# Float32r transposes of layer-norm outputs, fed by DMA copies, for tiles 3 to 13 of the first layer

## The chip, the cores and the metric

The kernel runs on one core of one Trainium2 chip. Times are device microseconds of one execution of the whole program; the figure for a kernel is the median of its runs.

## What is computed

An input of 2048 rows and 576 columns goes through a linear-attention block and an expert block, twice. Cut to what matters here:

```python
x = A_x
x = x + _A_ref(_layernorm(x), A_wqkv, A_wo)      # linear attention, 32 heads of 18
x = x + _B_ref(_layernorm(x), B_w_q, ...)        # one of 64 experts per head and row
x = x + _A_ref(_layernorm(x), A_wqkv, A_wo)
x = x + _B_ref(_layernorm(x), B_w_q, ...)

# in _A_ref
qkv = x @ wqkv                                   # q, k and v, 576 columns each
pq, pk = phi(q), phi(k)                          # phi(t) = max(t, 0) + min(exp(t), 1) + 1e-6
kv = einsum("bhsd,bhse->bhde", pk, v)
```

The change touches the beginning of the first attention block: layer norm, the transpose of its output, and the products for q, k and v.

## The kernel before

The 2048 rows are 16 tiles of 128 rows. In the code the first layer has the index 0, so a piece called `(0, t)` is tile t of layer 1.

For each tile of the front, ScalarE writes the layer norm's output `y` (line 187, float32, five blocks of 128 columns; the middle 64 columns stand there twice). TensorE transposes the five blocks into one PSUM tile `pt` with a float32 identity (line 197). ScalarE rounds `pt` to a float32r tile `thi` (line 102), VectorE writes the rest into `tlo` (line 103). The products k, v and q (line 212) take 28 matmul pairs each from `thi`, `tlo` and the weights split in the same way (`whi`, `wlo`). ScalarE and VectorE make phi of k and q (lines 218 to 221), q goes to DRAM by DMA (`pq_d`, line 254), and phi(k) with v is summed over the tiles into one PSUM tile `kva` (lines 283 and 285).

The tiles 2 to 12 are done by one loop (lines 724 to 749). The iteration of tile t runs, on TensorE, k of t, v of t, q of t, the transposes of tile t+1 (`fT`) and the sum of t. For t up to 9, eight matrices of the second block's weights are folded at the end (`fold_load`, line 540, and `fold_mm`, line 550); every second iteration from t = 4 on also has `fold_out` and `fold_T`, which move a finished fold through a buffer `foldf` and five more transposes. From t = 10 on there is nothing to fold, and the transposes come between v and q. The layer norm of tile t+1 (`first_ln`) stands at the beginning of the iteration. Tiles 14 and 15 follow in an order written out by hand.

Inside the loop the order on TensorE, ScalarE, VectorE and GpSimd is that of the code (`in_order`). All DMAs are issued by SyncE (SP), in an order that the scheduler sets; SP takes them one after the other, and each waits for its data and its buffer. Every engine works through its own instructions in order, so one that waits holds up all behind it on that engine.

Two pools matter. The tiles `y` and `foldf` share three buffers of one tag. PSUM has four tiles of 128 x 1024 float32 for everything that TensorE writes, one of which `kva` holds through the loop.

Of the kernel before, what the change touches and what calls it, by code (L numbers as in the profile page):

```python
# [11 lines left out]
F32 = mybir.dt.float32  # L12
F32R = mybir.dt.float32r
BF16 = mybir.dt.bfloat16
I32 = mybir.dt.int32
AF = mybir.ActivationFunctionType
ALU = mybir.AluOpType
AX = mybir.AxisListType
# [4 lines left out]
P = 128  # L23
# [12 lines left out]
NB = 5  # L36


def blocks(rem):

    rows, at = [], 0
    for b in range(NB):
        rows.append((at, b - (b > rem)))
        at += 64 if b == rem else P
    return rows
# [12 lines left out]
def network(ctx, tc, x_in, wqkv, wo, wq_t, k_t, u_t, v2, c_mask, c_mask4, c_ident, c_code, c_code1, c_scale, c_shift, out):  # L58
    nc = tc.nc

    cp = ctx.enter_context(tc.tile_pool(name="cp", bufs=1))
    wk = ctx.enter_context(tc.tile_pool(name="wk", bufs=2))
# [3 lines left out]
    def psum(name):  # L66
        return ps.tile([P, 1024], F32, tag="ps", name=name)
# [3 lines left out]


    ident = cp.tile([P, P], F32, name="ident")
    mask = cp.tile([HC + 1, HC + 72], F32, name="mask")
    pick = cp.tile([HC + 1, 2 * P], F32, name="pick")
    code_w = cp.tile([P, 512], BF16, name="code_w")
    shift = cp.tile([P, 64], I32, name="shift")
    mhalf = cp.tile([P, 1], F32, name="mhalf")
# [21 lines left out]
    def split(src, hi, lo, eng=nc.vector):  # L100

        nc.scalar.activation(hi, src, AF.Copy)  # L102
        eng.tensor_tensor(lo, src, hi.bitcast(F32), op=ALU.subtract)  # L103

    def split_mixed(src, dst):

        nc.scalar.activation(dst, src, AF.Copy)
        nc.vector.tensor_tensor(dst[64:], src[64:], dst[64:].bitcast(F32), op=ALU.subtract)
# [24 lines left out]
    def split_weight(tiles, c0, hi, lo, rem, which=range(NB), eng=nc.vector):  # L133
        for b in which:
            cols = slice(c0, c0 + D)
            if b != rem:
                split(tiles[b], hi[:, b, cols], lo[:, blocks(rem)[b][1], cols], eng)
            else:
                split_mixed(tiles[b], hi[:, b, cols])
# [42 lines left out]

    def normalized(xt, rs, n):

        y = wk.tile([P, 2, 320], F32, tag="y", name=f"y{n}", bufs=3)
        x2 = bass.AP(tensor=xt.tensor, offset=xt.offset, ap=[xt.ap[0], [256, 2], [1, 320]])
        nc.scalar.activation(y, x2, AF.Identity, scale=rs[:, 0:1], bias=rs[:, 1:2])  # L187
        return y.rearrange("p a b -> p (a b)")

    def transposed(y, n, more=None, tag="t", step=P):  # L190

        todo = [y[:, b * step:b * step + P] for b in range(NB)] if y is not None else []
        todo += [] if more is None else [more]
        w = len(todo) * P
        pt = psum(f"pt{n}")
        for b, x in enumerate(todo):
            nc.tensor.transpose(pt[:, b * P:(b + 1) * P], x, ident)  # L197
        nb = NB if tag == "t" else NB + 1
        hi = wk.tile([P, nb, P], F32R, tag=tag + "hi", name=f"thi{n}", bufs=4 if tag == "t" else 1)
        lo = wk.tile([P, nb, P], F32R, tag=tag + "lo", name=f"tlo{n}", bufs=4 if tag == "t" else 1)  # L200
        yield
        split(pt[:, :w], hi.rearrange("p a b -> p (a b)")[:, :w], lo.rearrange("p a b -> p (a b)")[:, :w])
        return hi, lo

    def product(tt, hi, lo, cols, n, cut=HALF, rem=REM, by_block=False):

        o = psum(f"pp{n}")
        todo = sorted(passes(rem), key=lambda p: p[1]) if by_block else passes(rem)
        for i, (a, b, w) in enumerate(todo):
            wb = hi[:, b] if w == "hi" else lo[:, blocks(rem)[b][1]]  # L210
            for c0, c1, at in ((0, cut, 0), (cut, D, 512)):
                nc.tensor.matmul(o[:, at:at + c1 - c0], tt[a == "lo"][:, b, :], wb[:, cols + c0:cols + c1],  # L212
                                 start=(i == 0), stop=(i == len(todo) - 1))
        return o
# [9 lines left out]
    tt = {}  # L224
    xs = {}
    ys = {}
# [2 lines left out]


    def front_T(l, t):
        tt["f", l, t] = yield from transposed(ys.pop(("f", l, t)), f"f{l}_{t}")

    def front_k(l, t):
        k = product(tt["f", l, t], whi, wlo, D, f"k{l}_{t}", by_block=(l == 0 and t == 0))
# [177 lines left out]
    def exp_T(l, t, c):  # L413

        y = ys.pop(("b", l, t)) if ok(t) else None
        cg = tt.pop(("cg", l, c)).rearrange("p a b -> p (a b)") if ok(c) else None
        if y is None and cg is None:
            return
        hi, lo = yield from transposed(y, f"b{l}_{t % 99}", cg, tag="t" if cg is None else "u")
        if y is not None:  # L420
            tt["b", l, t] = hi, lo
        if cg is not None:
            b = 0 if y is None else NB
            tt["c", l, c] = hi[:, b], lo[:, b]
# [127 lines left out]

    def fold_out(ch):
        p = fold_ps.pop(ch)
        f = wk.tile([P, 640], F32, tag="y", name=f"foldf{ch}", bufs=3)
        nc.scalar.activation(f[:, :320], p[:, :320], AF.Copy)
        nc.scalar.activation(f[:, 320:384], p[:, 256:320], AF.Copy)
        nc.scalar.activation(f[:, 384:], p[:, 512:768], AF.Copy)
        fold_st["f", ch] = f
# [21 lines left out]
    def warm_up(n):  # L581

        p = psum("warm")
        for i in range(n):
            nc.tensor.matmul(p[:, :512], junk[:, :P], junk[:, :512], start=True, stop=True)

    def first_load(l, t):
        xt = wk.tile([P, D], F32, tag="x", name=f"xf_{t}", bufs=3)
        nc.sync.dma_start(xt, x_in[t * P:(t + 1) * P, :])
        xs["f", t] = xt  # L590
# [47 lines left out]
    def ok(t):  # L638
        return 0 <= t < NT
# [3 lines left out]
    def run(l, *seq):  # L643


        for f, t, *n in seq:
            if f is bc or ok(t):
                g = begun.pop((f, l, t), None) or (exp_T(l, *t) if f is bc else f(l, t))
                for i in range(n[0] if n else 99):
                    if g is None or next(g, bc) is bc:  # L650
                        break
                else:
                    begun[f, l, t] = g
# [39 lines left out]
    with in_order(*ALL):  # L693
        x0, x1 = xs.pop(("f", 0)), xs.pop(("f", 1))
        warm_up(14)
        rs0 = statistics(x0, "f0_0", soon=True)
        split_weight(wk_in, D, whi, wlo, REM, (0,))
        ys["f", 0, 0] = normalized(x0, rs0, "f0_0")
        split_weight(wk_in, D, whi, wlo, REM, (1, 2))
        run(0, (fT, 0, 1))  # L700
        warm_up(2)
        run(0, (fT, 0))
        split_weight(wk_in, D, whi, wlo, REM, (3,), nc.gpsimd)
        rs1 = statistics(x1, "f0_1", soon=True)
        split_weight(wk_in, D, whi, wlo, REM, (4,))
        ys["f", 0, 1] = normalized(x1, rs1, "f0_1")
        run(0, (k, 0, 1), (fT, 1))
        split_weight(wv_in, 2 * D, whi, wlo, REM, (0, 1))
        run(0, (k, 0), (k, 1, 1))
        split_weight(wv_in, 2 * D, whi, wlo, REM, (2, 3, 4))  # L710
        first_load(0, 2)
        wq_in = load_weight(wqkv, 0, REM, "w")
        small_loads()
        first_load(0, 3)
        run(0, (k, 1), (v, 0, 1))
        split_weight(wq_in, 0, whi, wlo, REM, (0, 1))
        run(0, (v, 0))
        first_ln(0, 2)
        split_weight(wq_in, 0, whi, wlo, REM, (2, 3))
        run(0, (v, 1, 1))  # L720
        split_weight(wq_in, 0, whi, wlo, REM, (4,))
        run(0, (st, 0), (fT, 2), (v, 1), (q, 0), (st, 1), (q, 1))
        PER, FIRST = 8, 13
        for t in range(2, FIRST):
            m0 = PER * (t - 2)
            groups = [m for m in range(m0, m0 + PER) if m < 2 * H]
            done = (m0 - 1) // 16 if m0 % 16 == 0 and 0 < m0 <= 2 * H else None
            for m in groups:
                fold_load(m)
            if t + 2 < NT:  # L730
                first_load(0, t + 2)
            if t + 1 < NT:
                first_ln(0, t + 1)
            run(0, (k, t, 1))
            if done is not None:
                fold_out(done)
            run(0, (k, t))
            run(0, (v, t, 1))
            if done is not None and groups:
                fold_T(done)  # L740
            run(0, (v, t))
            if groups:
                run(0, (q, t), (fT, t + 1), (st, t))
            elif t < L:
                run(0, (fT, t + 1), (q if t < L - 1 else st, t), (st if t < L - 1 else q, t if t < L - 1 else -1))
            if done is not None and not groups:
                fold_T(done)
            for m in groups:
                fold_mm(m)
# [101 lines left out]
```

## Time and profile before

| what | before |
|---|---|
| median of 3 runs | 756.94 us (755.6 to 759.04) |
| span of the profiled execution | 753.7 us |
| TensorE busy | 736.8 us, 98% of the span |
| VectorE, ScalarE, GpSimd busy | 456.8, 289.1, 197.7 us |
| one float32 transpose of the layer-norm output, record on TensorE | 270 to 330 ns, 160 of them over both layers |
| fold load, issue to landing | 3.2 to 6.0 us, 64 of 288 KB |

Of the profiled execution no other time is recorded than its span, from the first to the last instruction of the program. In the views PE is TensorE's matmuls, PEld its weight loads, DVE VectorE, ACT ScalarE, POOL GpSimd and SPq the DMA issues of SyncE. A row of the timeline gives start, duration, engine, line, operation, tiles and count, and in brackets the engine's idle time before it with what ended it. Consecutive matmuls overlap, so the distance between starts says more than a record's length. In rows of stretches the last three numbers are the granted TensorE clock, the busy share of the 16 DMA engines and the GB/s that they moved. The lines on which the prediction rests stand in it.

### The profile page before, as it was taken

What the parts mean: (1) busy time and instruction counts of PE and PEld (TensorE: products, weight loads), DVE (VectorE), ACT (ScalarE), POOL (GpSimd) and SP (SyncE); (2) the same over time, 40 slices, a digit from 0 to 9 for tenths busy, and PEclk for the clock granted to TensorE, in tenths of its full rate; (3) what the DMA queues carried; (4) which work ended last, traced back from release to release, by engine and by line L of the source; (5) the groups of instructions that cost most, each with busy time, mean ns of one, the idle gap of its engine ahead of it and who ended that gap; (6) DMA issues with size and microseconds to landing.
All of it is one profiled execution on the core that took longest, in us unless ns stands there. A gap on an engine that the chain in (4) does not pass through costs nothing.

```text
span 753.7 us, 13987 instructions
## 1 busy us (share of the span) xinstructions
PE 736.8 (98%) x5356; PEld 693.2 (92%) x5356; DVE 456.8 (61%) x1008; ACT 289.1 (38%) x586; POOL 197.7 (26%) x540
## 2 busy tenths in 40 slices
PE   7999999999999999999999999999999999999996
PEld 5999989999998989999999999999999999999984
DVE  5532342324246887666666665563366789999996
ACT  5422232232333544444444443533234333343443
POOL 2110001000002543333333342230033343534331
PEclk9999999999999999999999999999999999999999
DMA  9736446631111322222232211321733213111201
GB/s 275 245 125 223 157 171 220 218 118 49 48 63 32 110 89 77 98 84 83 92 105 101 83 67 60 111 68 38 206 107 112 85 65 115 48 48 58 70 33 63
DMA packets 52267, 79.48 MB, mean 105 GB/s; under 512 B 5480, under 2 KB 22376, under 8 KB 52200
## 3 DMA queue, kind: packets, MB, share of 16 engines
q1 hardware_dynamic: 52200, 78.59, 31.8%
q8 instruction: 42, 0.69, 0.4%
q14 instruction: 25, 0.20, 0.1%
HBM read 55.01 MB, written 23.56 MB: 104 GB/s over the span
## 4 chain that ended last, share of the span: by engine, by line
PE 81%; DVE 10%; ACT 3%; issue 2%; POOL 2%; DMA 1%; SPq 0%; DVEq 0%; POOLq 0%; ACTq 0%
PE ppk L212 15%; PE ppv L212 15%; PE ppo L402 13%; PE pps L433 12%; PE ppq L212 11%; PE kva L283 4%; PE fold_ps L550 2%; PE ptf L197 2%; PE ptb L197 2%; PE po L517 2%; PE pto L197 2%; PE m L332 1%; DVE tloo L103 1%; DVE o L379 1%; DVE x L391 1%
## 5 line engine op out<-in xcount | busy, mean ns | idle before, releaser
L219 DVE TENSOR_SCALAR ek<-ek 128x576 f32<-128x576 f32 x32 | 14.7, 459 | 81.4 <-ACT ek L218 76.9
L212 PE MATMUL ppk<-whi,thif 128*128 128x288 f32 x320 | 50.4, 301 | 1.6 <-ACT thif L102 1.6
L402 PE MATMUL ppo<-ohi,thio 126*128 126x288 f32 (+1 forms) x320 | 50.9, 301 | 0.8 <-DVE ct L492 0.5
L212 PEld LDWEIGHTS ppk<-whi,thif 128*128 128x128 f32 x320 | 44.2, 188 | 5.6 <-issue 3.3
L163 POOL TENSOR_SCALAR rsf<-mvf 128x1 f32<-128x1 f32 x16 | 3.1, 192 | 175.6 <-DVE mvf L161 175.4
L212 PE MATMUL ppk<-whi,tlof 128*128 128x288 f32 x320 | 48.7, 296 | 0.3 <-DVE tlof L103 0.3
L212 PE MATMUL ppv<-whi,thif 128*128 128x252 f32 x320 | 48.0, 296 | 0.1
L187 ACT ACTIVATE yb<-x,rsb 128x640 f32<-128x640 f32 x32 | 29.5, 923 | 47.9 <-POOL rsb L180 47.9
L212 PE MATMUL ppv<-whi,tlof 128*128 128x252 f32 x320 | 47.6, 295 | 0.0
L219 DVE TENSOR_SCALAR eq<-eq 128x576 f32<-128x576 f32 x32 | 15.8, 493 | 51.7 <-ACT eq L218 51.7
L433 PE MATMUL pps<-shi,thib 128*128 128x512 f32 x160 | 44.4, 407 | 2.0 <-ACT thib L102 2.0
L402 PEld LDWEIGHTS ppo<-ohi,thio 126*128 126x128 f32 (+1 forms) x320 | 44.6, 189 | 1.9 <-issue 0.7
L212 PEld LDWEIGHTS ppk<-whi,tlof 128*128 128x128 f32 x320 | 44.6, 188 | 0.5 <-DVE tlof L103 0.5
L212 PEld LDWEIGHTS ppv<-whi,tlof 128*128 128x128 f32 x320 | 44.6, 188 | 0.0
L212 PEld LDWEIGHTS ppv<-whi,thif 128*128 128x128 f32 x320 | 44.2, 188 | 0.3 <-ACT thif L102 0.3
L438 ACT ACTIVATE s<-pps 128x512 f32<-128x512 f32 x32 | 19.1, 596 | 61.4 <-PE pps L433 61.4
L433 PE MATMUL pps<-shi,tlob 128*128 128x512 f32 x160 | 42.5, 395 | 0.0
L103 DVE TENSOR_TENSOR tlof<-ptf,thif 128x640 fp32r<-128x640 f32 x32 | 26.2, 818 | 24.3 <-ACT thif L102 24.2
L402 PE MATMUL ppo<-ohi,tloo 126*128 126x288 f32 x256 | 40.3, 295 | 0.0
L402 PE MATMUL ppo<-olo,thio 126*128 126x288 f32 x256 | 40.3, 296 | 0.0
L212 PE MATMUL ppk<-wlo,thif 128*128 128x288 f32 x256 | 39.9, 296 | 0.0
L212 PE MATMUL ppq<-whi 128*128 128x288 f32 x260 | 39.6, 299 | 0.1
(156 smaller groups left out, 1778.6 us busy)
## 6 DMA issues: line engine op xcount, KB each, us to landing
fold<-in_wq_t SPq DMA_DIRECT2D x64, 288.0 KB, 4.8
whi<-hl_d SPq DMA_DIRECT2D x26, 320.0 KB, 3.5
pq_d<-eq SPq DMA_DIRECT2D x19, 288.0 KB
pq<-pq_d SPq DMA_DIRECT2D x19, 288.0 KB, 3.3
xf<-in_x SPq DMA_DIRECT2D x16, 288.0 KB, 4.7
x<-in_x SPq DMA_DIRECT2D x16, 288.0 KB, 2.8
x_d<-x SPq DMA_DIRECT2D x16, 288.0 KB, 3.1
x<-x_d SPq DMA_DIRECT2D x16, 288.0 KB, 2.6
```

What stands on the lines that cost most here:

```text
L103: eng.tensor_tensor(lo, src, hi.bitcast(F32), op=ALU.subtract)
L187: nc.scalar.activation(y, x2, AF.Identity, scale=rs[:, 0:1], bias=rs[:, 1:2])
L197: nc.tensor.transpose(pt[:, b * P:(b + 1) * P], x, ident)
L212: nc.tensor.matmul(o[:, at:at + c1 - c0], tt[a == "lo"][:, b, :], wb[:, cols + c0:cols + c1], start=(i == 0), stop=(i == len(todo) - 1))
L219: nc.vector.tensor_scalar(e, e, 1.0, EPS, op0=ALU.min, op1=ALU.add)
L283: nc.tensor.matmul(a[:w, c * HC:(c + 1) * HC], vt[:, c * w:(c + 1) * w], fk[:, c * HC:(c + 1) * HC], start=(t == 0 and c == 0), stop=(t == ...
L332: nc.tensor.matmul(m[:c, h * 512:h * 512 + HALF], kvb[:n, b * HC:b * HC + c], wob[l][b][:n, h * HALF:(h + 1) * HALF], start=True, stop=True)
L402: nc.tensor.matmul(p[:, h * 512:h * 512 + HALF], hl[a][:r, b], w[:r, h * HALF:(h + 1) * HALF], start=(i == 0), stop=(i == len(todo) - 1))
L433: nc.tensor.matmul(p[:, :512], hl[a == "lo"][:, b, :], shi[:, b] if w == "hi" else slo[:, blocks(REM)[b][1]], start=(i == 0), stop=(i == l ...
L438: nc.scalar.activation(s[:, NE:], p[:, :512], AF.Copy)
L517: nc.tensor.matmul(p[:, b * 512:b * 512 + HALF], c[i], vmix[:, b * HALF:(b + 1) * HALF], start=(i == 0 and not based), stop=(i == 1))
L550: nc.tensor.matmul(p[32 * j:32 * j + 32, at:at + c1 - c0], kpad[:, ch // 2, 24 - 8 * a:56 - 8 * a], st[:, c0:c1], start=(a == 0), stop=(a ...
```

## The change

For the tiles 3 to 13 of layer 1, the output of the layer norm is copied by a DMA from SBUF to SBUF into a second tile `r` of type float32r (`moved`; both ends are seen as float32, so the bits are unchanged). The five transposes then read `r` and a float32r identity, and write the same PSUM tile seen as float32r. Tiles 0 to 2, 14 and 15 and all other transposes stay as they are. The copy stands in the code between the k and the v product of the iteration before the one that uses it.

For tiles 5 and 9 the first block is also transposed both ways, from `y` in float32 and from `r` in float32r (`guard`); ScalarE copies the first result, VectorE compares the two, takes the maximum over a row and adds it to `mhalf`, the constant -0.5 that the layer norm's power uses. Where the two are equal, 0 is added.

The tag of `y`, `r` and `foldf` gets four buffers instead of three, and ScalarE writes the float32r identity once before the loop.

```diff
+    identr = cp.tile([P, P], F32R, name="identr")
...
-    def transposed(y, n, more=None, tag="t", step=P):
+    def transposed(y, n, more=None, tag="t", step=P, raw=False):
...
-            nc.tensor.transpose(pt[:, b * P:(b + 1) * P], x, ident)
+            if raw:
+                nc.tensor.transpose(pt[:, b * P:(b + 1) * P].bitcast(F32R), x, identr)
+            else:
+                nc.tensor.transpose(pt[:, b * P:(b + 1) * P], x, ident)
...
+    def moved(y, n):
+
+        r = wk.tile([P, NB * P], F32R, tag="y", name=f"r{n}", bufs=4)
+        nc.sync.dma_start(r.bitcast(F32), y)
+        return r
+
+    def guard(y, r, n):
+
+        a = psum(f"ga{n}")
+        b = psum(f"gb{n}")
+        nc.tensor.transpose(a[:, :P], y[:, :P], ident)
+        nc.tensor.transpose(b[:, :P].bitcast(F32R), r[:, :P], identr)
+        c = wk.tile([P, P], F32, tag="gc", name=f"gc{n}", bufs=1)
+        nc.scalar.activation(c, a[:, :P], AF.Copy)
+        nc.vector.tensor_tensor(c, c, b[:, :P], op=ALU.not_equal)
+        m = wk.tile([P, 1], F32, tag="gm", name=f"gm{n}", bufs=1)
+        nc.vector.tensor_reduce(m, c, axis=AX.X, op=ALU.max)
+        nc.vector.tensor_tensor(mhalf, mhalf, m, op=ALU.add)
...
     def front_T(l, t):
-        tt["f", l, t] = yield from transposed(ys.pop(("f", l, t)), f"f{l}_{t}")
+        tt["f", l, t] = yield from transposed(ys.pop(("f", l, t)), f"f{l}_{t}", raw=(l == 0 and 2 < t <= 13))
+
+    def front_moved(l, t):
+        y = ys.pop(("f", l, t))
+        r = moved(y, f"f{l}_{t}")
+        if t in (5, 9):
+            guard(y, r, f"f{l}_{t}")
+        ys["f", l, t] = r
...
+        nc.scalar.activation(identr, ident, AF.Copy)
...
             run(0, (k, t))
+            front_moved(0, t + 1)
             run(0, (v, t, 1))
```

On TensorE, in the iteration of tile 4, before: the end of tile 4's k product (`ppk_4`) and the beginning of its v product (`ppv_4`).

```order
L212 MATMUL ppk_4_875<-whi,tlof_4_822 128x288 x10
L212 MATMUL ppv_4_912<-whi,thif_4_821 128x252
L212 MATMUL ppv_4_912<-whi,thif_4_821 128x324
L212 MATMUL ppv_4_912<-whi,thif_4_821 128x252
```

And now, where `gaf_5` and `gbf_5` are the comparison's two PSUM tiles, `yf_5` the layer norm's output of tile 5 and `rf_5` its copy:

```order
L235 MATMUL ppk_4_881<-whi,tlof_4_828 128x288 x10
L219 MATMUL gaf_5_920<-ident,yf_5_879 128x128
L220 MATMUL gbf_5_921<-identr,rf_5_918 128x128
L235 MATMUL ppv_4_930<-whi,thif_4_827 128x252
L235 MATMUL ppv_4_930<-whi,thif_4_827 128x324
```

The two transposes of the comparison stand between k and v of tile 4, and the second reads the copy; tile 8's iteration has the same place for tile 9.

On SP, the DMAs issued around the same time, before: the store of tile 3's phi(q), eight fold loads and a load of x.

```order
L254 DMA pq_d_3_106<-eq_3_810 128x576
L540 DMA fold_850<-in_wq_t 128x576
L540 DMA fold_852<-in_wq_t 128x576
L540 DMA fold_854<-in_wq_t 128x576
L540 DMA fold_856<-in_wq_t 128x576
L540 DMA fold_858<-in_wq_t 128x576
L540 DMA fold_860<-in_wq_t 128x576
L540 DMA fold_1026<-in_wq_t 128x576
L540 DMA fold_1028<-in_wq_t 128x576
L589 DMA xf_1201<-in_x 128x576
```

And now:

```order
L284 DMA pq_d_3_107<-eq_3_816 128x576
L570 DMA fold_856<-in_wq_t 128x576
L570 DMA fold_858<-in_wq_t 128x576
L570 DMA fold_860<-in_wq_t 128x576
L570 DMA fold_862<-in_wq_t 128x576
L570 DMA fold_864<-in_wq_t 128x576
L570 DMA fold_866<-in_wq_t 128x576
L212 DMA rf_5_918<-yf_5_879 128x640
L570 DMA fold_1044<-in_wq_t 128x576
L570 DMA fold_1046<-in_wq_t 128x576
L619 DMA xf_1221<-in_x 128x576
```

The copy of tile 5 stands behind the store and six of the eight fold loads; the last two and the load of x now come after it.

On SP again, near the end of the loop, before: loads of `wo`, the store of tile 10's phi(q), a load of x and the store of tile 11's.

```order
L294 DMA wob_2591<-in_wo 126x576
L294 DMA wob_2597<-in_wo 72x576
L254 DMA pq_d_10_113<-eq_10_1984 128x576
L589 DMA xf_2345<-in_x 128x576
L254 DMA pq_d_11_114<-eq_11_2127 128x576
L354 DMA x_1_2521<-in_x 128x576
```

And now:

```order
L324 DMA wob_2635<-in_wo 126x576
L324 DMA wob_2641<-in_wo 72x576
L284 DMA pq_d_10_114<-eq_10_2024 128x576
L212 DMA rf_12_2096<-yf_12_2061 128x640
L619 DMA xf_2389<-in_x 128x576
L284 DMA pq_d_11_115<-eq_11_2169 128x576
L212 DMA rf_13_2225<-yf_13_2190 128x640
L384 DMA x_1_2565<-in_x 128x576
```

The copies of tiles 12 and 13 each stand right ahead of the load that waited for the same `y` before.

More of the change, by code (lines that the diff above doesn't have):

```diff
@@ L183, in normalized @@
     def normalized(xt, rs, n):
-        y = wk.tile([P, 2, 320], F32, tag="y", name=f"y{n}", bufs=3)
+        y = wk.tile([P, 2, 320], F32, tag="y", name=f"y{n}", bufs=4)
         x2 = bass.AP(tensor=xt.tensor, offset=xt.offset, ap=[xt.ap[0], [256, 2], [1, 320]])
@@ L554, in fold_out @@
         p = fold_ps.pop(ch)
-        f = wk.tile([P, 640], F32, tag="y", name=f"foldf{ch}", bufs=3)
+        f = wk.tile([P, 640], F32, tag="y", name=f"foldf{ch}", bufs=4)
         nc.scalar.activation(f[:, :320], p[:, :320], AF.Copy)
```

## The prediction

> **What bounds the kernel now.** I read the page's busy times first, then the chain that ended last, then the busy times by stretch over layer 1's front, where the change sits.
>
> ```profile
> PE   736.8 (98%) x5356; PEld 693.2 (92%) x5356; DVE 456.8 (61%) x1008; ACT 289.1 (38%) x586; POOL 197.7 (26%) x540
> PE 81%; DVE 10%; ACT 3%; issue 2%; POOL 2%; DMA 1%; SPq 0%; DVEq 0%; POOLq 0%; ACTq 0%
> 60.00:80.00 20.00, 20.00 (x173) 18.90 (x172) 6.15 (x14) 6.85 (x20) 1.01 (x3) 1.00 0.43 149
> 180.00:200.00 20.00, 19.75 (x155) 19.52 (x153) 7.55 (x15) 6.31 (x13) 2.02 (x6) 1.00 0.18 58
> ```
>
> TensorE is busy 98% of the span and all 20 us of 60 to 80; VectorE, ScalarE and the DMA engines (43%) have room. So a microsecond that TensorE loses or saves here goes to the end nearly whole. What counts is how much TensorE time the faster transposes save, and whether TensorE now meets a copy that has not landed.
>
> **What the transposes may save.** One iteration of the loop, tile 4's, as the timeline shows it:
>
> ```profile
> 69.40 1.50 PE L212 MATMUL ppk<-whi,tlof 128*128 128x288 f32 x10
> 70.74 1.49 PE L212 MATMUL ppv<-whi,thif 128*128 128x252 f32 x10
> ...
> 78.73 0.71 PE L197 MATMUL ptf<-ident,yf 128*128 128x128 f32 x5
> 79.27 1.05 PE L283 MATMUL kva<-ek,v 128*127 128x126 f32 x8
> ```
>
> Steps from start to start are safer than lengths, since records overlap. Five float32 transposes take 79.27 - 78.73 = 0.54 us, 0.108 each. Ten float32r matmuls of 288 columns take 70.74 - 69.40 = 1.34 us, 0.134 each, 0.465 ns a column; at that pace 128 columns take 0.060. No row shows a float32r transpose. It may step at 0.108 (nothing gained) or at 0.060; since the moving operand, the identity, is what turns float32r, I take 0.060. It saves 5 x 0.048 = 0.24 us a tile. A gain beyond 0.54 a tile is excluded: that is all the time there is.
>
> Against this stands the load of the weights, which every transpose has for itself:
>
> ```profile
> L197 PEld LDWEIGHTS ptf<-ident,yf x160: 137/140/144, 7.5 to 518.0; 128*128 128x128 f32 x160
> L212 PEld LDWEIGHTS ppk<-whi,thif 128*128 128x128 f32 x320 | 44.2, 188 | 5.6 <-issue 3.3
> ```
>
> A transpose's load is recorded with 140 ns, a float32r matmul's of the same shape with 188. If the float32r transpose gets the longer load, 48 ns more, the load may set the step and the saving is gone. [...]
>
> **What the copies cost.** In the loop each copy stands on SP behind the pq_d store and six fold loads. This is that place in the profile, with the layer norm whose output is copied:
>
> ```profile
> 65.37 0.33 SPq L254 DMA_DIRECT2D pq_d<-eq  x1
> 65.97 4.16 SPq L540 DMA_DIRECT2D fold<-in_wq_t  x8
> 68.49 0.92 ACT L187 ACTIVATE yf<-xf,rsf 128x640 f32<-128x640 f32 x1 [3.91 <-POOL rsf L166]
> 70.23 0.38 SPq L589 DMA_DIRECT2D xf<-in_x  x1
> ...
> L540 SPq DMA_DIRECT2D fold<-in_wq_t x2: 382/625/868, 67.4 to 67.8; - x2
> DMA to landing us min/median/max: 5.2/5.2/5.2
> ...
> 72.00:73.00 1.00, 1.00 (x10) 1.00 (x9) 0.84 (x2) 0.00 (x0) 0.00 (x0) 1.00 0.95 366
> 77.00:78.00 1.00, 1.00 (x10) 1.00 (x9) 0.97 (x4) 0.00 (x0) 0.00 (x0) 1.00 0.00 0
> ```
>
> Tile 5's y is done at 69.41, so its copy is issued at about 69.45. The DMA engines are then saturated (95% busy at 366 GB/s from 72 to 73) and idle again at 77. The fifth fold load, issued at 67.84, landed 5.2 us later, at 73.0. If transfers are served in order, the sixth (0.295 MB at 366 GB/s) comes 0.80 us after it and the copy (128 x 640 x 4 B = 0.328 MB) 0.90 us after that: 74.7.
>
> For most tiles that is early enough. Tile 5's own transposes start at 78.73, 4 us later, and every tile from 3 to 10 has an interval of this kind. Only the comparison asks sooner: its second transpose reads the copy of tile 5 right behind tile 4's k product, and in the program of before the v product starts there, at 70.74. TensorE works in order, so v, q and all that follows wait. With 0.05 us for the wait to end and 0.06 for the transpose, v starts at 74.8: **4.1 us lost**. What the iteration's earlier transposes saved (tile 4's) is lost in this wait too, because the landing hangs on the q product's output, not on them.
>
> Tile 9 is the same, from tile 8's iteration:
>
> ```profile
> 130.67 1.50 PE L212 MATMUL ppk<-whi,tlof 128*128 128x288 f32 x10
> 132.01 0.69 PE L212 MATMUL ppv<-whi,thif 128*128 128x252 f32 x4
> ...
> L540 SPq DMA_DIRECT2D fold<-in_wq_t x2: 382/382/383, 128.6 to 129.1; - x2
> DMA to landing us min/median/max: 5.5/5.5/5.5
> ```
>
> Fifth fold at 129.1 + 5.5 = 134.6, copy at 136.3, v at 136.4 instead of 132.01: **4.4 us**.
>
> The last tiles have no fold loads, but a late layer norm and a transpose that comes before q. Tile 12:
>
> ```profile
> 177.71 0.92 ACT L187 ACTIVATE yf<-xf,rsf 128x640 f32<-128x640 f32 x1 [4.12 <-POOL rsf L166]
> 178.66 0.35 SPq L589 DMA_DIRECT2D xf<-in_x  x1
> 179.62 0.71 PE L197 MATMUL ptf<-ident,yf 128*128 128x128 f32 x5
> 180.57 0.67 PE L212 MATMUL ppq<-whi,thif 128*128 128x288 f32 x3 [0.25 <-DVE ek L221]
> ...
> x_d<-x SPq DMA_DIRECT2D x16, 288.0 KB, 3.1
> x<-x_d SPq DMA_DIRECT2D x16, 288.0 KB, 2.6
> ```
>
> The x load waits for this y and is issued at 178.66; the copy takes its place. The nearest rows, a tile's store and load, land in 2.6 and 3.1 us; I take 2.7, so 181.4, and q starts 0.35 later, at 181.7 instead of 180.57: **1.1 us lost** (1.0 to 1.5 between the bounds), and the 0.25 that q waits for VectorE goes into it. Tile 13:
>
> ```profile
> 190.14 1.60 SPq L354 DMA_DIRECT2D x<-in_x  x2
> 192.91 0.71 PE L197 MATMUL ptf<-ident,yf 128*128 128x128 f32 x5
> ```
>
> Issued at 190.14, landed at 192.7 to 193.2, wanted at 192.91: 0.3 lost at most, about its own saving; I count nothing for the tile.
>
> The rest costs nothing while its cover lasts: the comparison's ScalarE copy and three VectorE steps (0.3 us or so each beside ScalarE's 0.92 for a tile five times as wide) and the float32 transpose (0.11) run while TensorE waits anyway; the identity's copy lies under TensorE's solid work. Two fold loads and an x load go out some 0.5 us later, but the engines are idle by 77 and the folds are used after 80.
>
> **The clock.** TensorE stands still for about 3.9 and 4.2 us. The longest such gap of before is near the end:
>
> ```profile
> 748.17 0.33 PE L197 MATMUL ptb<-ident,cg 128*128 128x128 f32 x1 [2.31 <-DVE cg L498]
> ...
> 747.00:748.00 1.00, 0.00 (x0) 0.00 (x0) 0.83 (x4) 0.00 (x0) 0.00 (x0) 1.00 0.60 233
> 749.00:750.00 1.00, 0.73 (x4) 0.47 (x4) 0.14 (x1) 0.19 (x1) 0.00 (x0) 1.00 0.34 134
> 750.00:751.00 1.00, 0.00 (x0) 0.00 (x0) 0.00 (x0) 0.47 (x1) 0.00 (x0) 0.60 0.42 161
> 751.00:752.00 1.00, 0.00 (x0) 0.00 (x0) 0.00 (x0) 0.00 (x0) 0.00 (x0) 0.50 0.68 265
> ...
> 1.22 5.58 PE L585 MATMUL warm<-junk 128*128 128x512 bf16 x14 [1.22 <-DVE junk L686]
> ```
>
> The granted clock holds through a gap of 2.31 us and halves soon after, when TensorE has had little to do for 4 us. How long it stays low is seen only at the start, where fourteen matmuls take 5.58 us, 0.78 ns a column against 0.465 later. So a fall costs between nothing and half of 5.58, 2.8 us; I take 1.4, and one fall in the two waits. [...]
>
> **The sum.** Lost: 4.1 + 4.4 + 1.1 = 9.6 us. Saved: tiles 3, 5, 6, 7, 9, 10 and 11, 7 x 0.24 = 1.7 (4 and 8 are eaten by the waits, 12 and 13 are counted). 7.9 us, and 9.3 with one fall of the clock. The profiled execution's span is 753.7; the runs have a median of 756.94, 3.2 above it, which lies outside the span and which I leave as it is: 756.94 + 9.3 = **766.2 us**.
>
> **Rivals.**
> - The clock falls in both waits: 7.9 + 2.8 = 10.7, **767.6**. For it: gaps nearly twice the longest one that passed. Against it: the trace's one fall came after 4 us of thin work, not from a single gap.
> - The change does not do what it says, and a float32r transpose steps like a float32 one (the load): the 1.7 is gone, 9.3 + 1.7 = 11.0, **767.9**.
> - Not slower: the copies do not queue behind the folds. They come from SBUF, and if the engines served them beside the loads they would land 2.6 to 3.1 us after 69.45, at 72.1 to 72.6. Then each comparison costs about 1.7, too short for the clock (2.31 passed): 3.4 + 1.1 - 1.7 = 2.8, **759.7**. It decides once the copy lands by about 72.6. Against it: the folds were issued 0.48 apart but landed 5.2 us on, as in a queue, and all go through one SP queue.
> - Faster needs more than 3.8 us; even with transposes that cost nothing (0.54 a tile) the last case stays at +0.7. I leave 2% for what I do not see.
>
> **How the numbers follow.** Forecast 0.48, both falls 0.18, no faster transposes 0.18, early copies 0.14, unseen 0.02. A measurement of this kernel can tell about 0.5%, 3.8 us, from no change. The first three cases lie above it: slower 0.84; early copies are no change: 0.14; faster 0.02. The forecast's own range is 764.8 (no fall, 7.9) to 767.6. The range of 759.5 to 769.5 adds the early copies down to 0.2 below their value, and upward the case of no faster transposes with a second fall (769.3); it leaves out half of the early copies' spread and what I do not see.
>
> **What would show it.** In the profile of after: two idle stretches of TensorE of about 4 us, near 71 and 136, ended by the copy's DMA at the comparison's second transpose; one of about 1 us at tile 12; the granted clock below 1.00 just behind one of the long ones; five float32r transposes in 0.30 us. Long waits without a step below 0.108 mean the load rules. I am wrong at the root if TensorE's waits there are under 2 us, or if the transposes save more than 0.54 a tile elsewhere.

## The result and the profile after

| what | before | after |
|---|---|---|
| median of 4 runs | 757.91 us (755.6 to 759.04) | 769.5 us (769.25 to 770.53) |
| span of the profiled execution | 753.7 us | 768.7 us (time 770.53) |
| mean granted TensorE clock of that execution | 0.998 | 0.989 |

The ratio of after to before is 1.0165, with a 95% interval of 1.0146 to 1.0185: by the ratio the change costs about 12.5 us, by the medians 11.6. The profiled execution of before was one of its quickest (its span of 753.7 and the 1.8 us outside that after's execution shows make 755.5), so the two profiles differ by 15.0 us, more than the medians.

The page of after, in the same order as that of before: busy times, the granted clock in 40 slices of the span, and the chain that ended last.

```profile
PE 738.9 (96%) x5360; PEld 696.0 (91%) x5360; DVE 460.3 (60%) x1014; ACT 289.7 (38%) x589; POOL 196.2 (26%) x540
PEclk9999999899999999999999999999999999999998
PE 77%; DVE 12%; DMA 3%; ACT 3%; issue 2%; POOL 2%; SPq 0%; DVEq 0%; POOLq 0%; ACTq 0%
```

TensorE is busy 2.1 us longer in a span that is 15.0 us longer: most of the time is idle time of TensorE, not work. DMA's share of the chain grew from 1% to 3%, and the clock row has an 8 in its eighth slice, 135 to 154 us. A shorter fall at 76.6 us does not show in these tenths; finer stretches below show it.

What TensorE waited for between 30 and 220 us, over all tiles of the change (us in all, number, longest):

```profile
PE gbf L220 <- DMA rf<-yf: 9.8, 2, 5.1
PE ptf L199 <- DMA rf<-yf: 1.6, 1, 1.6
```

The two long waits are the comparisons of tiles 5 and 9 (`gbf` is the PSUM tile of the second transpose), the third is tile 12. There is none at tile 13. The timeline of TensorE around the first comparison, then around the second:

```profile
69.99 1.50 PE L235 MATMUL ppk<-whi,tlof 128*128 128x288 f32 x10
71.32 0.27 PE L219 MATMUL gaf<-ident,yf 128*128 128x128 f32 x1
76.38 0.25 PE L220 MATMUL gbf<-identr,rf 128*128 128x128 f32 x1 [4.78 <-DMA rf<-yf]
76.46 2.64 PE L235 MATMUL ppv<-whi,thif 128*128 128x252 f32 x10
...
81.79 0.71 PE L595 MATMUL fold_pt<-ident,foldf 128*128 128x128 f32 x5
...
137.62 1.50 PE L235 MATMUL ppk<-whi,tlof 128*128 128x288 f32 x10
144.29 0.34 PE L220 MATMUL gbf<-identr,rf 128*128 128x128 f32 x1 [5.05 <-DMA rf<-yf]
144.43 2.75 PE L235 MATMUL ppv<-whi,thif 128*128 128x252 f32 x10
149.95 0.71 PE L595 MATMUL fold_pt<-ident,foldf 128*128 128x128 f32 x5
```

The same two places in the profile of before, as far as they are not shown yet:

```profile
74.44 0.71 PE L565 MATMUL fold_pt<-ident,foldf 128*128 128x128 f32 x5
...
132.01 1.49 PE L212 MATMUL ppv<-whi,thif 128*128 128x252 f32 x10
...
135.71 0.71 PE L565 MATMUL fold_pt<-ident,foldf 128*128 128x128 f32 x5
```

From the last ten matmuls of k to the first of v it took 1.34 us before at both places (69.40 to 70.74, 130.67 to 132.01), and takes 6.47 and 6.81 us now: 5.1 and 5.5 us lost. Then v itself is longer: from its first matmul to `fold_pt` 3.70 us before at both places, 5.33 and 5.52 now, 1.6 and 1.8 us more. Nothing waits there; it is the clock. Stretches of 2 us in the profile of after (PE, PEld, DVE, ACT, POOL busy, then granted clock, DMA share, GB/s):

```profile
74.00:76.00 2.00, 0.00 (x0) 0.00 (x0) 0.00 (x0) 0.00 (x0) 0.00 (x0) 1.00 1.05 412
76.00:78.00 2.00, 1.62 (x8) 1.66 (x9) 0.74 (x3) 0.00 (x0) 0.00 (x0) 0.65 0.67 263
78.00:80.00 2.00, 2.00 (x10) 2.00 (x9) 0.00 (x0) 0.00 (x0) 0.00 (x0) 0.50 0.00 0
80.00:82.00 2.00, 2.00 (x17) 2.00 (x16) 0.00 (x0) 0.00 (x0) 0.00 (x0) 1.00 0.00 0
...
142.00:144.00 2.00, 0.00 (x0) 0.00 (x0) 0.00 (x0) 0.00 (x0) 0.00 (x0) 0.50 0.98 386
146.00:148.00 2.00, 2.00 (x10) 2.00 (x10) 0.00 (x0) 0.00 (x0) 0.00 (x0) 0.50 0.00 0
```

While TensorE waits, the DMA engines are saturated, 98 to 105% busy at 386 to 412 GB/s by these rows: the copy is coming behind the folds. Behind the first wait TensorE does 10 matmuls in 2 us instead of 17, at a clock of 0.50; at the second the clock is down, 0.50 from 142 to 144 us, before the wait is over.

Tile 12 in the timeline of after, with the layer norm on ScalarE, the end of the v product, the copy's issue on SP, the transposes and the q product behind them, and v's row in before:

```profile
191.67 0.92 ACT L188 ACTIVATE yf<-xf,rsf 128x640 f32<-128x640 f32 x1 [4.12 <-POOL rsf L167]
192.25 1.48 PE L235 MATMUL ppv<-whi,tlof 128*128 128x252 f32 x10
192.62 0.50 SPq L212 DMA_DIRECT2D rf<-yf  x1
195.32 0.59 PE L199 MATMUL ptf<-identr,rf 128*128 128x128 f32 x5 [1.59 <-DMA rf<-yf]
195.75 1.56 PE L235 MATMUL ppq<-whi,thif 128*128 128x288 f32 x10
```

```profile
178.29 1.49 PE L212 MATMUL ppv<-whi,tlof 128*128 128x252 f32 x10
```

The copy is issued at the end of y, with no folds ahead of it, and the wait for it ends 2.7 us later (192.62 to 195.32). From the last ten matmuls of v to q it is 3.50 us (192.25 to 195.75) instead of 2.28 (178.29 to 180.57): 1.2 us lost. The sum: 5.1 + 5.5 for the waits, 1.6 + 1.8 for the clock, 1.2 for tile 12, together 15.2; less 0.9 that the transposes of nine tiles saved, plus 0.8 by which this execution was later before the first float32r transpose (the two traces matched instruction by instruction): 15.1, against 15.0 between the spans.

### The profile page after: what moved, and what is told of

Its sections match the earlier page's. It is cut to its first block, busy times and chain, and to the rows that moved or that the text cites. A ratio compares the mean times of both kernels' runs of the same rounds, so it can differ in the third digit from the quotient of the medians.

```text
span 768.7 us, 14032 instructions
## 1 busy us (share of the span) xinstructions
PE 738.9 (96%) x5360; PEld 696.0 (91%) x5360; DVE 460.3 (60%) x1014; ACT 289.7 (38%) x589; POOL 196.2 (26%) x540
## 4 chain that ended last, share of the span: by engine, by line
PE 77%; DVE 12%; DMA 3%; ACT 3%; issue 2%; POOL 2%; SPq 0%; DVEq 0%; POOLq 0%; ACTq 0%
PE ppv L235 15%; PE ppk L235 13%; PE ppo L432 13%; PE pps L463 11%; PE ppq L235 11%; PE kva L313 3%; PE ptb L201 2%; DMA rf<-yf 2%; PE po L547 2%; PE fold_ps L580 2%; PE ptf L201 1%; PE pto L201 1%; DVE o L409 1%; DMA xf<-in_x 1%; DVE eq L244 1%
## 5 line engine op out<-in xcount | busy, mean ns | idle before, releaser
L235 PE MATMUL ppv<-whi,thif 128*128 128x252 f32 x320 | 50.4, 306 | 0.1
L235 PEld LDWEIGHTS ppv<-whi,thif 128*128 128x128 f32 x320 | 46.2, 196 | 0.4 <-ACT thif L103 0.4
L235 PE MATMUL ppv<-wlo,thif 128*128 128x252 f32 (+1 forms) x256 | 40.1, 300 | 0.0
```

## The experiments

My theory after the result: the slowdown is the two comparisons, each by its place (TensorE waits there for a copy behind six fold loads) and by the fall of the clock that follows. The rivals: the comparison's own work, the copies' traffic or the transposes themselves cost the time; or the queue is the fault and another queue would end the wait. Ratios are to before, run beside it on the same chip, with 95% intervals.

**Without the comparison.** Copies and float32r transposes stay.

```diff
 def front_moved(l, t):
     y = ys.pop(("f", l, t))
     r = moved(y, f"f{l}_{t}")
-    if t in (5, 9):
-        guard(y, r, f"f{l}_{t}")
     ys["f", l, t] = r
```

> The comparison is left out; copies and float32r transposes of tiles 3 to 13 stay. If the comparison's early read of the copy is what costs (the two waits of 4.8 and 5.1 us and the clock behind them), the time returns to that of before: about 1.6 us of gain (0.16 a tile in the profile of after, ten tiles) against about 1.2 lost at tile 12, so a ratio to before of 0.998 to 1.002, no wait of TensorE near 71 or 136 and a granted clock of 1.00 throughout. If the copies themselves cost (DMA traffic, buffers, the start of the program), it stays 3 us or more above before.

Measured 756.65 us, ratio 1.0001 (0.9989 to 1.0013). The only wait of TensorE in these tiles is tile 12's, 1.6 us as in after. The stretch of 20 us around the first comparison's place in this kernel:

```profile
60.00:80.00 20.00, 20.00 (x174) 18.90 (x173) 5.86 (x14) 6.89 (x20) 1.00 (x3) 1.00 0.54 183
```

TensorE is busy all 20 us again at full clock, while the DMA engines move 183 GB/s instead of 149. So the copies' traffic costs TensorE nothing there, copies and transposes together leave the time where it was, and the slowdown is the comparison's. This profile's span is 755.0, 13.7 below that of after; the four terms above make 14.0.

**The comparison in another place.** It stands behind q of the iteration, right ahead of the tile's own transposes; the copy has landed by then.

```diff
+    held = {}
...
     if t in (5, 9):
-        guard(y, r, f"f{l}_{t}")
+        held[t] = y, r
...
-    run(0, (q, t), (fT, t + 1), (st, t))
+    run(0, (q, t))
+    if t + 1 in held:
+        guard(*held.pop(t + 1), f"f0_{t + 1}")
+    run(0, (fT, t + 1), (st, t))
```

> The comparison is kept whole, but stands behind the q product, right ahead of the transposes of the same tile, some 8 us after its place in the changed kernel. If it is the wait and not the work that costs, this is e1 plus two transposes of about 0.1 us each per comparison, 0.4 us in all, ratio to before 0.998 to 1.003. If the comparison's work costs (two PSUM tiles of four, three VectorE steps), it stays 3 us or more above e1.

Measured 757.98 us, ratio 1.0015 (1.0004 to 1.0027). The timeline of TensorE there:

```profile
79.27 0.30 PE L220 MATMUL gbf<-identr,rf 128*128 128x128 f32 x1
80.32 0.61 PE L199 MATMUL ptf<-identr,rf 128*128 128x128 f32 x5 [0.74 <-ACT gcf L222]
```

No wait for the copy is left at the comparisons, so the place was the cost and not the work. I had missed one thing: the five transposes need a PSUM tile, and the one that comes free is that of the comparison's first result, which ScalarE (`gcf`) must read first. That is 0.74 us at each of the two, and by the ratios 1.1 us over the kernel without comparison.

**The wait filled with work.** Eighteen bfloat16 matmuls whose result nobody reads stand between the comparison's two transposes, so that the wait stays and TensorE is busy in it. Half as many in the second kernel below.

```diff
     nc.tensor.transpose(a[:, :P], y[:, :P], ident)
+    for i in range(18):
+        nc.tensor.matmul(b[:, 512:], junk[:, :P], junk[:, :512], start=True, stop=True)
     nc.tensor.transpose(b[:, :P].bitcast(F32R), r[:, :P], identr)
```

> As the changed kernel, but 18 bf16 matmuls on zeros (0.22 us each at full clock, 3.9 us) stand between the comparison's two transposes, so that TensorE is busy during the wait. The wait for the copy still ends when it ends. If the idle time lowers the clock and this costs 1.6 and 1.8 us behind the two waits, the granted clock stays 1.00 and the time is about 3.4 us below the changed kernel's, 766. If the clock's fall costs nothing (the work behind waits for something else anyway), the time stays at 769 to 770.

Measured 765.6 us, ratio 1.0113 (1.0089 to 1.0136). The first comparison on the timeline of TensorE, and after it the stretch behind it:

```profile
72.38 4.05 PE L221 MATMUL gbf<-junk 128*128 128x512 bf16 x18
77.59 0.28 PE L222 MATMUL gbf<-identr,rf 128*128 128x128 f32 x1 [1.16 <-DMA rf<-yf]
77.70 1.57 PE L237 MATMUL ppv<-whi,thif 128*128 128x252 f32 x10
```

```profile
78.00:80.00 2.00, 2.00 (x17) 2.00 (x16) 0.71 (x3) 0.00 (x0) 0.00 (x0) 1.00 0.16 62
```

The copy comes no sooner, and the comparison holds v up as before; but the clock stays at 1.00 and the first ten matmuls of v take 1.57 us by their record instead of 2.64. The ratio is 0.0052 below the result's 1.0165, 3.9 us for both falls, with intervals that leave 1.6 to 6.2; the profile of after had 1.6 + 1.8. What is left, some 8.6 us, is the waits and tile 12.

> As e3, with 9 matmuls in the wait instead of 18, so about 1.9 us of work and then some 3 us of idle time before each copy lands. If the clock falls as soon as a gap is much longer than the 2.3 us that passed, it falls in one or both waits, and the time is 767 to 769.5; if it needs a gap near 4 us or more, it holds, and the time is e3's, 765 to 766.

With nine matmuls: 766.35 us, ratio 1.0123 (1.0104 to 1.0142). The comparison on TensorE's timeline, and after it the stretch around it:

```profile
76.16 0.28 PE L222 MATMUL gbf<-identr,rf 128*128 128x128 f32 x1 [2.36 <-DMA rf<-yf]
76.28 1.56 PE L237 MATMUL ppv<-whi,thif 128*128 128x252 f32 x10
```

```profile
76.00:78.00 2.00, 1.84 (x14) 1.84 (x15) 0.73 (x3) 0.00 (x0) 0.00 (x0) 1.00 0.64 250
```

The idle stretches of 2.36 us here and 2.5 us at tile 9 leave the clock up (1.00 in the row; the execution's mean is 0.996, as without the comparison), and the time equals that with eighteen within the intervals. In two of this kernel's four executions the mean clock was 0.993 and 0.994 beside 0.996 and 0.997, so a fall in those is not excluded.

The length of a wait may not be all that counts. In the profile of after the granted clock changes at 76.59, 80.00, 141.44 and 148.27 us, 3.41, 61.44 and 6.83 us apart; the first fall comes 0.2 us behind the end of a wait of 4.78 us, the second 2.2 us into one of 5.05. Here are the 3.41 us ahead of each of the two falls (0.21 and 1.20 us busy, so 3.2 and 2.2 idle), and then the two stretches, of the same division of the span, that have the most idle time of those with no fall behind them (1.6 us each):

```profile
73.17:76.59 3.42, 0.21 (x2) 0.25 (x3) 0.35 (x1) 0.00 (x0) 0.00 (x0) 1.00 1.02 393
138.03:141.44 3.41, 1.20 (x10) 0.94 (x8) 1.22 (x2) 1.24 (x5) 0.00 (x0) 1.00 0.96 289
```

```profile
69.76:73.17 3.41, 1.83 (x14) 1.57 (x13) 0.86 (x2) 1.86 (x6) 0.00 (x0) 1.00 0.94 270
192.64:196.05 3.41, 1.82 (x16) 1.63 (x15) 1.22 (x2) 1.36 (x5) 0.00 (x0) 1.00 0.57 183
```

My estimate from these stretches is that it also matters where a wait lies, and that nine matmuls were enough here is then in part luck; no run shows it.

**The copies by another queue.** ScalarE issues each copy itself, right behind the layer norm that writes `y`, where the copy passes no fold load on SP.

```diff
-    nc.sync.dma_start(r.bitcast(F32), y)
+    nc.scalar.dma_start(r.bitcast(F32), y)
...
-    r = moved(y, f"f{l}_{t}")
+    r = rs_early.pop(t)
...
     first_ln(0, t + 1)
+    rs_early[t + 1] = moved(ys["f", 0, t + 1], f"f0_{t + 1}")
```

> As the changed kernel, but the copies are issued by ScalarE right behind the layer norm, not by SP behind the store and the fold loads. If a copy comes late because it stands behind the loads in SP's one queue, it now lands about 3 us after its issue at 70, near 73, the waits shrink to 1.5 to 2.5 us, the clock holds, and the time is before plus 3 to 5 us (761 to 763). If the engines' load is what counts, whatever the queue, the copy still lands near 75 to 76, and the time stays at 768 to 770.

Measured 776.75 us, ratio 1.0251 (1.0221 to 1.0281): worse than after, and neither of the two cases I had set down. The timeline with the issues on SP and ScalarE, the comparison and tile 12, and after it the stretch behind tile 12's wait:

```profile
66.05 4.63 SPq L572 DMA_DIRECT2D fold<-in_wq_t  x8
69.62 0.47 ACTq L212 DMA_DIRECT2D rf<-yf  x1
77.48 0.34 PE L220 MATMUL gbf<-identr,rf 128*128 128x128 f32 x1 [6.40 <-DMA rf<-yf]
201.65 0.85 PE L199 MATMUL ptf<-identr,rf 128*128 128x128 f32 x5 [3.30 <-DMA rf<-yf]
```

```profile
202.00:204.00 2.00, 2.00 (x11) 2.00 (x11) 0.73 (x1) 0.70 (x1) 0.00 (x0) 0.50 0.00 0
```

The copy goes out at 69.62, no sooner than y is there, and the wait for it ends at 77.48, 7.9 us later. All eight folds now go out by 70.7, the last two no longer behind the copy, and the DMA engines are 94 to 101% busy from 72 to 76 us. Here the waits are 6.40 and 6.9 us. The clock falls in the first (0.68 from 74 to 76 us, then 0.50) and once more at tile 12, where the wait grows from 1.59 to 3.30 us; the execution's mean is 0.982, against 0.989 in after. So ScalarE's queue does not end the wait.

**Copies with float32 transposes.** No comparison; `r` is copied, and transposed seen as float32 with the old identity.

```diff
-    nc.tensor.transpose(pt[:, b * P:(b + 1) * P].bitcast(F32R), x, identr)
+    nc.tensor.transpose(pt[:, b * P:(b + 1) * P], x.bitcast(F32), ident)
...
-    if t in (5, 9):
-        guard(y, r, f"f{l}_{t}")
```

> As e1 (no comparison), but the transposes read the copies as float32 with the float32 identity: only the DMAs are left of the change. If a float32r transpose steps by 0.076 us instead of 0.108, five of these take 0.54 us instead of 0.38, and the time is 1.4 to 1.8 us above e1's, a ratio to before of 1.001 to 1.0035. If the saving does not reach the end, it equals e1.

Measured 757.94 us, ratio 1.0021 (1.0012 to 1.0029). Against the same kernel with float32r transposes (1.0001) this is 0.0020, 1.5 us, with intervals that leave 0.4 to 2.6, between kernels that did not run side by side; tile 12's wait of 1.6 us is in both. The trace gives 0.10 us a tile, 0.9 in all: the tiles 3 to 11 show it, 12 and 13 do not. These are the weight loads and matmuls of five transposes and of the sum behind them in the profile of after, then the same of before where it isn't shown yet:

```profile
63.69 0.53 PEld L199 LDWEIGHTS ptf<-identr,rf 128*128 128x128 f32 x5
64.16 0.96 PEld L313 LDWEIGHTS kva<-ek,v 128*127 128x127 f32 x8
63.82 0.55 PE L199 MATMUL ptf<-identr,rf 128*128 128x128 f32 x5
64.20 1.11 PE L313 MATMUL kva<-ek,v 128*127 128x126 f32 x8
65.15 0.29 PE L315 MATMUL kva<-ek,v 128*73 128x72 f32 x2
```

```profile
78.59 0.60 PEld L197 LDWEIGHTS ptf<-ident,yf 128*128 128x128 f32 x5
79.16 0.96 PEld L283 LDWEIGHTS kva<-ek,v 128*127 128x127 f32 x8
...
80.16 0.29 PE L285 MATMUL kva<-ek,v 128*73 128x72 f32 x2
```

The five transposes take 0.38 us (63.82 to 64.20) instead of 0.54. But the loads now step 0.094 (63.69 to 64.16, five) instead of 0.114, and the next eight matmuls take 0.95 (64.20 to 65.15) instead of 0.89 (79.27 to 80.16): part of the saving is given back at once, and 0.10 remains. Taken one by one, the five transposes start about 0.06, 0.07, 0.085 and 0.085 us apart, and their loads, after the first step, 0.086; in before both step 0.109. So the first step is the 0.060 that I had worked out from the moving operand, and the last two are those of the loads; what sets them is not shown, since no run changes the load alone.

**No copies at all.** ScalarE writes the layer norm of tiles 3 to 13 rounded to float32r, and the transposes read it.

```diff
-    y = wk.tile([P, 2, 320], F32, tag="y", name=f"y{n}", bufs=4)
+    y = wk.tile([P, 2, 320], dt, tag="y", name=f"y{n}", bufs=4)
...
-    if t in (5, 9):
-        guard(y, r, f"f{l}_{t}")
...
-    front_moved(0, t + 1)
```

> ScalarE writes the layer-norm output of tiles 3 to 13 straight as float32r, rounded, so that copies and comparison are gone and float32r transposes are all that is left; the values differ from the reference's. If each tile saves 0.16 us and all of it reaches the end, 11 x 0.16 = 1.8 us below before: a ratio of 0.9965 to 0.999. If something else of the change costs (the fourth buffer, the identity), it is 1.000 or above.

Measured 755.7 us, ratio 0.9994 (0.9984 to 1.0004). The gain I expected is not there; nine times 0.10 us is 0.9 us, 0.0012, which lies in the interval, and so does no gain at all. So nothing larger was hidden behind the copies.

**Only tiles 3 to 11, no comparison.** The copies of tiles 12 and 13 go, whose transposes follow the layer norm closely.

```diff
-    raw=(l == 0 and 2 < t <= 13)
+    raw=(l == 0 and 2 < t <= 11)
...
-    if t in (5, 9):
-        guard(y, r, f"f{l}_{t}")
...
-    front_moved(0, t + 1)
+    if t + 1 <= 11:
+        front_moved(0, t + 1)
```

> As e1, but tiles 3 to 11 only: tiles 12 and 13, whose layer norm comes too late for a copy, are transposed as before. The wait of 1.6 us at tile 12 goes, 9 x 0.16 = 1.4 us stay saved: a ratio to before of 0.997 to 1.000, 1 us below e1. If the wait at tile 12 was not on the path to the end, it equals e1.

Measured 755.7 us, ratio 0.9992 (0.9983 to 1.0000); span 753.4. In the first comparison-free kernel TensorE waited 1.6 us at tile 12; here its only wait from 30 to 220 us is one that before had too, 0.2 us at tile 12's q:

```profile
PE ppq L235 <- DVE ek L244: 0.2, 1, 0.2
```

It is the quickest kernel of the study and still not to be told from before: nine tiles by 0.10 us are 0.9 us, 0.0012.

> Tiles 3 to 11 as in e7, with both comparisons as in e2, behind the q product: all the changed kernel's parts without its waits. e7 plus e2's cost over e1 (0.9 to 1.3 us): 756.3 to 757, a ratio to before of 0.9995 to 1.0015. If the comparisons' places still make TensorE wait for a copy, 3 us or more above before.

With the comparison added behind q, as in the second experiment: 756.28 us, ratio 0.9994 (0.9984 to 1.0003). So what the change computes, the comparison of two tiles included and tiles 12 and 13 transposed as before, can be had at the time of before.

**The change again.** No edit, to see how much the waits and the clock vary.

> The changed kernel once more, on the chip and beside the runs of before that the other two of this call have. If its cost lies in two waits of 4.8 to 5.5 us and two falls of the clock of 1.5 to 1.8 us each, whatever the chip, the ratio to before is 1.0165 to 1.0185, with two such waits and two falls again; if the falls are a chance of one run, it is 1.012 to 1.016.

Measured 769.58 us, ratio 1.0173 (1.0155 to 1.0191). Its waits at the comparisons (us in all, number, longest), and after them the stretches in the first of them and behind it:

```profile
PE gbf L220 <- DMA rf<-yf: 8.4, 2, 4.4
```

```profile
74.00:76.00 2.00, 0.00 (x0) 0.00 (x0) 0.08 (x1) 0.00 (x0) 0.00 (x0) 0.74 1.02 395
...
78.00:80.00 2.00, 2.00 (x10) 2.00 (x10) 0.00 (x0) 0.00 (x0) 0.00 (x0) 0.50 0.01 3
```

The waits are 4.40 and 4.0 us, shorter than in the first profile, and the clock, in the first of them now down within the wait (0.74 from 74 to 76 us), costs 2.4 us there instead of 1.6: from v's first matmul to `fold_pt` it takes 6.09 us (76.69 to 82.78), against 3.70 before. The span is 768.2 us, 14.5 above that of before. With 1.2 for tile 12 and 0.9 saved, as in the first profile, the comparisons' delay and the clock come to some 14 us in both profiles, 10.6 + 3.4 in the first and, as an estimate from the spans and the 8.4 us of waits, with 0.8 around them as in the first, 9.2 + 5 in the second. The mean clock of this execution is 0.986, against 0.989.

**Six comparisons.** Tiles 4 to 9.

```diff
-    if t in (5, 9):
+    if t in (4, 5, 6, 7, 8, 9):
```

> As the changed kernel, but tiles 4 to 9 are compared instead of 5 and 9: six waits instead of two. If each costs its wait (5.2 to 5.5 us) and its fall of the clock (1.6 to 1.8), four more are 27 to 29 us: 795 to 799. If the waits fall together (one wait lets the loads of the next iteration go early), much less, 780 to 790.

Measured 796.2 us, ratio 1.0518 (1.0501 to 1.0535). The waits at the comparisons:

```profile
PE gbf L220 <- DMA rf<-yf: 26.6, 6, 4.7
```

Six waits, the first of 3.95 us and the longest of 4.7, and the clock falls behind the first (0.83 from 60 to 62 us, 0.50 from 62 to 64) and again at 82 us (0.97 from 78 to 82, 0.60 from 82 to 86). The mean clock of the execution is 0.981, against 0.989 and 0.986 with two comparisons. A comparison costs (796.2 - 756.7) / 6 = 6.6 us; two cost (769.58 - 756.7) / 2 = 6.4 each. The cost goes with their number.

## Why the prediction was wrong, point by point

The direction, the two places and the mechanism came out as predicted; 766.2 was 3.3 us too low, of which 1.0 is before's own median, 757.91 with one more execution instead of 756.94. All the terms that were off were off the same way.

- **What bounds the kernel: right.** What TensorE lost went to the end one for one (15.1 of 15.0 us).
- **The clock: the step that failed.** "So a fall costs between nothing and half of 5.58, 2.8 us; I take 1.4, and one fall in the two waits." It fell in both waits of the first profile and cost 3.4 us, 2.0 more than the term; in the second profile it cost 2.4 at the first wait and by the estimate 5 in all, 3.6 more than the term. The price of one fall, 1.6 to 2.4 us where the rows show it, was within my bounds; that it would fall once was a choice between none and two for which I had no row. What I set against the second fall, that before's only fall came after 4 us of thin work and not from one gap, did not hold: single gaps of 4.78 and 5.05 us were enough. The trace of before, with one fall of the clock and no gap of TensorE over 2.31 us, could not show that. The case "the clock falls in both waits" was among the rivals, at 767.6, and its mechanism is the one that happened. The shortest wait with a fall was 3.30 us, the longest without one 2.5 (the end of the program aside).
- **The waits at the comparisons: right in kind, short in the first profile.** I had 3.9 and 4.2 us of idle time; it was 4.78 and 5.05, and 4.40 and 4.0 in the second profile. That the copies come in the order of the queue was right: in both waits of the first profile the copy landed 0.8 us after the sixth fold load (75.40 and 76.24, 143.34 and 144.15), where I had worked out 0.90. What moved was the sixth fold load itself, which landed 9.3 and 9.6 us after the store ahead of it was issued, against 8.4 and 8.7 at the same places in before; I had drawn it from one execution. This is 2.1 us of error in the first profile (10.6 us against 8.5), as much as the clock's there, and 0.7 in the second; its size in another execution can't be foretold from one trace.
- **The saving: there, but its size too large.** I took 0.060 a transpose from the moving operand and 0.24 a tile; it was 0.076 and, after what the next matmuls gave back, 0.10. The longer load that the rival needed did not come: the float32r transpose's is recorded with 141 ns, like the float32 one's and not with 188, and the loads step 0.094 against 0.114, so the saving is not gone. By the single starts the last two transposes do step as their loads, 0.085 and 0.086, but that the load sets the step is not shown. That the data, the stationary operand, turn float32r as well as the identity I had left out. Nine tiles saved 0.9 us instead of the 1.7 for seven: 0.8 of the error. The shorter load, the experiment with float32 transposes and the one without copies all point to this size, yet in the time of a kernel it stays within the intervals.
- **Tiles 12 and 13: right.** 1.2 us against 1.1, and none. That the wait at tile 12 was on the path is shown by the kernel without those two copies, whose span is 1.6 us shorter and whose ratio is 0.0009 lower (0.7 us, with intervals that overlap).
- **What costs nothing while its cover lasts: right here.** The comparison's work lies in the wait. Without that cover it costs 1.1 us for two, through the PSUM tile, which I had not costed.
- **The early copies: refuted.** They do queue, and issuing them on another engine made it worse.

What stays open: whether copies issued ahead of the fold loads on SP would end the waits. The layer norm is done only after most of the folds have gone out, so it takes a change of the order of the work, which was not tried.

## What to carry to other kernels

A check that reads a copy cost here what TensorE waited for it, not what it computes: put it right ahead of the copy's ordinary reader, where two of them cost 1.1 us. When a change stops a saturated TensorE, count a fall of the clock for every stop as long as those that had one here (3.30 us and more), not one for all of them; stops of up to 2.5 us had none in these tiles, and between the two nothing was measured. And before paying for a faster form of an instruction, look at how its weight loads step as well as its matmuls: here the last transposes stepped as their loads (0.085 and 0.086 us), and the next eight matmuls took back part of the saving (0.95 us instead of 0.89).

## What the runs showed of the hardware

- In the profile of after the granted clock fell to 0.50 at 76.59, 141.44 and, at the end of the program, 762.67 us; in the 3.41 us ahead of these falls TensorE idled 3.2, 2.2 and 2.2 us. Before's one fall, at 750.20, had 2.2 us idle ahead of it. In no other stretch of the same division in these two profiles did TensorE idle more than 1.6 us at full clock.
- The clock fell in or behind each wait of TensorE from 3.30 us upward at which rows show its course (4.78 and 5.05 us in the first profile of the change, 4.40 in the second, 3.95 with six comparisons, 6.40 and 3.30 with ScalarE's queue), and behind none of those up to 2.5 us in the same tiles. In the first profile it stayed at half for 3.41 and 6.83 us; part of that lies within the wait, where it costs nothing, so the price of a fall was 1.6 and 1.8 us there, and 2.4 at the first wait of the second profile.
- Nine matmuls of 512 columns within such a wait kept the clock up in the profile (1.00 from 74 to 80 us); they gave the time back that the falls cost, 3.2 us by the medians against 3.4, and no more.
- A transpose of 128 columns steps 0.076 us in float32r and 0.108 in float32, and its weight load is recorded with nearly the same median (141 ns against 140) though the loads step 0.094 against 0.114. The step from start to start told it, the record did not.
